# Moving the global-by-global scores of an attention kernel into the spare columns of another score bank

## The chip, the cores and the metric

The kernel runs on one core of a Trainium2 chip. The metric is the device time of one execution in microseconds. An execution of this kernel is one launch that takes 64 attention heads and a gated feed-forward layer from inputs in HBM to outputs in HBM. The core's engines are named as in the profile: PE does matrix multiplies (its weight loads have their own row, PEld), DVE and ACT do elementwise work and can read PSUM, POOL does elementwise work in SBUF only, and SP issues DMAs.

## The reference

There are 8 batches of 8 heads, 512 local tokens, 32 global tokens and a head dimension of 64. A local token attends to the 32 global keys and to local keys within 32 positions. A global token attends to all 32 + 512 keys. The result is a token's input to a gated feed-forward layer of 512 to 1536 to 512.

```python
k_all = np.concatenate([k_g, k_l], axis=2)
s_g = scale * np.matmul(q_g, k_all.transpose(0, 1, 3, 2))   # global queries: 32 x 544 scores a head
out_g = np.matmul(sm(s_g), v_all)
...
mask = np.abs(pos[:, None] - pos[None, :]) <= window        # local queries: a band, plus the globals
s_l = np.concatenate([s_lg, s_ll], axis=-1)
out_l = np.matmul(sm(s_l), v_all)
...
gate = 1.0 / (1.0 + np.exp(-(x @ w_gate)))
return gate * (x @ w_val) @ w_out
```

## The kernel before, in words

Everything is computed to float32 accuracy. Operands are split into a high and a low float32r part (`qk_hi` and `kl`, `vhl`, `xt`, `hh`), and a product takes two or three matmuls. Weights come as float64 words and are converted at the start (`convert`).

The work is cut into chunks of tokens: two half chunks of batch 0, then one chunk of 512 local tokens for each of the batches 1 to 7, and at last the global tokens of all batches. The feed-forward of one chunk (`ffn_stream`) walks over 12 blocks of the hidden dimension. A block has 12 matmuls into `bank_g`, 12 into `bank_v` and 12 into the output banks `bank_o`. Between groups of these matmuls runs the attention of the next chunk, so attention of the chunks for batches 2 to 7 (six of them) runs under a steady feed-forward, and attention of batch 0 and 1 runs at the start, among the weight conversion.

A head of a full chunk has three attention units: `local_unit` for query blocks 0 and 1, `local_unit` for query blocks 2 and 3 (the second local unit), and `global_unit`. Each unit has four stages:

- Local: scores into a bank `bank_x` of shape [128, 2, 256], of which a block uses 224 columns (`WIN`); mask and row maximum on DVE (line 237), exponent on ACT (line 240). Then the normalisation into `p_buf` on DVE (line 213). Then four transposes on PE into `bank_y` (line 254), whose two float32r parts are made by ACT (line 263) and DVE (line 264, the tile `pt`). Then the product with the values (lines 280 and 281), and `t0` and the sum of parts on ACT, DVE and POOL.
- Global: scores with the local keys into `sa`, a `bank_x` of [32, 4, 128] (line 299), and scores with the 32 global keys into `sb`, a `bank_y` of its own of [32, 32] (line 301). DVE takes the row maximum of both (lines 304 and 305) and combines them (line 306), ACT takes the exponents of both (lines 308 and 309) into `pg_buf`, DVE scales it (lines 311 to 313), PE transposes it (line 317).

The feed-forward's own elementwise work for a block of the hidden dimension: tanh of `bank_g` on ACT (line 370), minimum on DVE (375), absolute value (377) and exponent (376) on ACT, `th` from two SBUF operands on DVE (378), times `bank_v` on DVE (380), the split of `hh` on ACT (382) and POOL (383). The split of the next heads' queries and keys is a cast on ACT (193) and three subtractions on POOL (194 and 196).

PSUM has eight banks. Four hold `bank_o`. The other four are one pool, which `bank_x`, `bank_y`, `bank_g` and `bank_v` share:

```python
acc = ps.tile([P, 512], F32, name=nm, tag="att", bufs=4)[:, 0:ntok]
s_ps = ps.tile([P, 2, 256], F32, name="bank_x", tag="att", bufs=4)
sb = ps.tile([32, 32], F32, name="bank_y", tag="att", bufs=4)
```

A tile of the pool gets its bank when an earlier tile's last reader is done, and PE waits for that reader.

The order of the work comes from two things. The driver emits stages of attention by ticks of the feed-forward (one tick is four matmuls of 512 columns): units follow each other every 4 ticks and a unit's stages lie 3 ticks apart. A block of the hidden dimension has 9 ticks and a head has 12, so the position of a head within the feed-forward repeats every three heads; from tick 8 of a chunk on everything is put off by one tick. From what is emitted the framework makes each engine's queue, in an order that it plans when the program is built. An engine works through its queue strictly in that order.

Of the kernel before, what the change touches and what calls it, by code (L numbers as in the profile page):

```python
# [8 lines left out]
F32 = mybir.dt.float32  # L9
# [11 lines left out]
SG = 32  # L21
NH = 8
# [4 lines left out]
QK = Q1 + 256 + SG  # L27
VM = (0, 1, 4, 5)
VS = (2, 3, 6, 7)
WIN = 224  # L30
DM = 512

# Where work is issued, in ticks of the feed-forward (one tick is four 512-token
# matmuls). Attention units of a chunk follow each other every PER ticks; a unit's
# stages lie STAGES apart, its operands are loaded and split ahead of it.
BASE, PER = 3, 4
STAGES = (0, 3, 6, 9)
LOAD_QK, LOAD_V, SPLIT_QK, SPLIT_V = 16, 9, 10, 4
LOAD_V_NATIVE = 4
# from the first of these ticks of a chunk on, attention is put off by the second  # L40
HOLE = (8, 1)
START = dict(per0=4, base1=1, per1=1.1, base2=23, per2=3, x2=28, lead=8, native_heads=4)
CONVERT = (-2, 4, 1, 3)
CONVERT_EARLY = (-985, -980, -977)
# the engines that share a kind of operation in turn: v(ector), s(calar)
NORM = {0: "v", 1: "v", 2: "ssv", 3: "sv"}
# [4 lines left out]
KT = DM // P  # L51
# [3 lines left out]
def kernel(ctx, tc, qk, v, w_gate, w_val, w_out, out_l, out_g):  # L55
    nc = tc.nc
# [4 lines left out]
    const = ctx.enter_context(tc.tile_pool(name="const", bufs=1))  # L61
    raw = ctx.enter_context(tc.tile_pool(name="raw", bufs=1))
    spl = ctx.enter_context(tc.tile_pool(name="spl", bufs=2))
    att = ctx.enter_context(tc.tile_pool(name="att", bufs=2))
# [5 lines left out]

# [1 line left out]
    ident = const.tile([P, P], F32, name="ident")  # L72
# [3 lines left out]
    nc.gpsimd.memset(masks[:, 1], 0.0)  # L76
    # window column c < 96 stands for key c - 32, c >= 128 for key c - 64
    # (relative to the block's first query); the columns between are global
    mid = masks[:, 1]
    for c0, lo, hi in ((0, 0, 64), (128, 96, -32)):  # L80
        cols = mid[:, c0:c0 + 96]
# [12 lines left out]
    pg = const.tile([32, 5 * P], F32, name="pg_buf")  # L94
    nc.vector.memset(pg, 0.0)
    xg32 = const.tile([P, KT, NG], F32, name="xg32")

# [1 line left out]
    wg = [const.tile([P, KT, DF], F32R, name=f"wg{i}") for i in range(2)]  # L99
# [19 lines left out]
    def convert(i, hi, lo):  # L119
        """The two float32r parts of a float64 [128, KT or 1, n] block, given as words."""  # L120
        src = w_src[i]
        t, n = src.shape[1], src.shape[2] // 2
        st, v = (o[i % len(o)].rearrange("p (t n) -> p t n", t=t) for o in conv_bufs)
        words = st.rearrange("p t (n two) -> p t n two", two=2)
        low, high = words[:, :, :, 0], words[:, :, :, 1]
        vf, hf = v.bitcast(F32), high.bitcast(F32)
        with tc.issue_after(anchor[0].ins) if i < 3 else nullcontext():
            nc.vector.tensor_scalar(v, high, 0x80000000, None, op0=ALU.bitwise_and)
            # read as a float32, the high word times 2^-112 has its exponent rebased to
            # float32's, with zeros between the sign and the exponent's eight bits  # L130
            if REBASE[i % len(REBASE)] == "s":
                nc.scalar.mul(hf, hf, 2.0 ** -112)
            else:
                nc.vector.tensor_scalar(hf, hf, 2.0 ** -112, None, op0=ALU.mult)
            nc.vector.scalar_tensor_tensor(v, low, 29, v, op0=ALU.logical_shift_right, op1=ALU.bitwise_or)
            nc.vector.scalar_tensor_tensor(v, high, 3, v, op0=ALU.logical_shift_left, op1=ALU.bitwise_or)
        nc.scalar.copy(hi, vf)
        nc.gpsimd.tensor_tensor(lo, vf, hi.bitcast(F32), op=ALU.subtract)
        stage(i + len(conv_bufs[0]))
# [11 lines left out]

# [1 line left out]
    def qcol(j):  # L153
# [62 lines left out]
    def local_unit(T, blocks, x32s, h, col0):  # L216
        ks, k0s, q0 = T["qk"], T["k0"], T["q0"]
        nat = T["native"]
        last = len(ks) - 1
        s_ps = ps.tile([P, 2, 256], F32, name="bank_x", tag="att", bufs=4)  # L220
        for i, j in enumerate(blocks):
            qj = ks[0][:, qcol(j) - q0:qcol(j) - q0 + P]
            for t, (kt, k0) in enumerate(zip(ks, k0s)):
                js = slice(k0 + j * BLK, k0 + j * BLK + WIN)
                nc.tensor.matmul(s_ps[:, i, 0:WIN], qj, kt[:, js], start=t == 0, stop=t == last)  # L225
# [9 lines left out]
        for i, j in enumerate(blocks):  # L235
            m = 0 if j == 0 else (2 if j == 3 else 1)
            anchor[0] = nc.vector.tensor_tensor_reduce(  # L237
                out=s_sb[:, i], in0=s_ps[:, i, 0:WIN], in1=masks[:, m], scale=-0.125, scalar=3.0e38,
                op0=ALU.add, op1=ALU.min, accum_out=nm[:, i:i + 1])
            nc.scalar.activation(s_sb[:, i], s_sb[:, i], AF.Exp, bias=nm[:, i:i + 1], scale=-1.0,  # L240
                                 accum_out=sm[:, i:i + 1])
        yield
        nc.vector.tensor_scalar_add(r, sm, 1e-9)  # L243
# [43 lines left out]
    def global_unit(T, b, h):  # L287
# [5 lines left out]
        sa = ps.tile([32, 4, P], F32, name="bank_x", tag="att", bufs=4)  # L293
        sb = ps.tile([32, 32], F32, name="bank_y", tag="att", bufs=4)
        for half in range(2):
            o0 = 96 * half
            for t, (src, k0) in enumerate(zip(ks, k0s)):
                view = src[:, k0 + 32:k0 + 32 + 4 * BLK].rearrange("p (j c) -> p j c", c=BLK)[:, :, o0:o0 + 64]
                nc.tensor.matmul(sa[:, :, 64 * half:64 * half + 64], qg, view, start=t == 0, stop=t == last)  # L299
        for t, (src, k0) in enumerate(zip(ks, k0s)):  # L300
            nc.tensor.matmul(sb, qg, src[:, k0 + 96:k0 + 128], start=t == 0, stop=t == last)  # L301
        mg = small.tile([32, 4], F32, name="mg")
# [35 lines left out]

# [1 line left out]
    hl_q = []  # L340
# [6 lines left out]
    def ffn_stream(items):  # L347
        """Items (chunk, block of the hidden dimension); yields the part of a full
        512-token step that was issued, between groups of matmuls."""
        prev = None  # L350
# [57 lines left out]

    # ---- driver: attention of the next chunk runs between the matmul groups
    def att_events(ci, start, per, tail=0):  # L410
        """(tick, order, thunk) of all attention work for chunk ci."""
        b, blocks, with_g = chunks[ci]
# [8 lines left out]
        for h in range(NH):  # L421
            native = ci + 1 if ci < 2 or (ci == 2 and h < START["native_heads"]) else 0
            place = (spl, "qk_hi", QK)
            if ci == 0 and h >= 4:
                place = (spl, "kl", KEXT)
            if ci == 1 and h // 2 == 2:
                place = (raw, "qk_raw", QK)
            heads.append(dict(first=ci == 0, native=native, h=h, n=b * NH + h, cols=slice(c0, c1),
                              wins=slice(0, 8 if with_g else 4), group=group, place=place))
# [38 lines left out]
    chs.append(dict(ntok=NG, x0=0, o0=0, first=False, xt=lambda: xts[G], dst=out_g))  # L468
    # the first two half chunks share the steps in which the weights are converted
    lead = START["lead"]  # L470
# [5 lines left out]

    # events on the feed-forward's clock: one tick is four 512-token matmuls
    queue = att_events(0, -1000, START["per0"]) + att_events(1, START["base1"], START["per1"])
# [85 lines left out]
```

## Time and profile before

| | |
|---|---|
| median of 3 runs | 1266.98 us (1265.59 to 1267.98) |
| span of the profiled execution | 1265.6 us |
| PE busy | 1221.5 us, 97% |
| DVE, ACT, POOL busy | 877.6 us (69%), 783.3 us (62%), 570.6 us (45%) |
| start, until attention of batch 1 is done | about 270 us |
| a steady chunk | 139.2 us, six of them with attention |
| the last full chunk, feed-forward alone, and the global tokens | about 160 us |

The span is the profiled execution's own time; it lies 1.4 us below the median. In the views that follow a row of the timeline gives start and duration in us, engine, line, operation, what is written and read, the shape, and in brackets the idle time of the engine before it with what ended it. A busy PE is not a PE at its peak: its matmuls are pipelined, so the distance between two starts tells what a matmul costs.

### The profile page before, as it was taken

Reading aid. Unit: us, or ns where it says so; the run is one execution under the profiler, and the core shown is the slowest. Engines: PE = TensorE matmul, PEld = TensorE weight load, DVE = VectorE, ACT = ScalarE, POOL = GpSimd, SP = SyncE. Lnnn points to the kernel's source line nnn. Section 1 sums busy time; section 2 is a strip of 40 time slices with the busy share of each in tenths; the row PEclk is TensorE's granted clock in tenths of the full one; section 3 lists DMA queues with packets and bytes.
Section 4 is the critical chain, followed back from the end, with each engine's and each line's share of the span. In section 5 each row is a group of like instructions: output and inputs, shape, how many; then the busy total and the mean of one; then the engine's idle time right before and its main releaser. Section 6 shows DMA issues by size and latency. Waiting matters only on the chain.

```text
span 1265.6 us, 20474 instructions
## 1 busy us (share of the span) xinstructions
PE 1221.5 (97%) x6820; PEld 994.1 (79%) x6820; DVE 877.6 (69%) x2433; ACT 783.3 (62%) x1899; POOL 570.6 (45%) x573
## 2 busy tenths in 40 slices
PE   5899989999999999999999999999999999999998
PEld 4676768788788877888788877888788877888897
DVE  4797976757877777857876778767775787632232
ACT  4586766756666666666666667756765766532233
POOL 1444554545555355545555455535554555311111
PEclk9698999999999999999999999999999999999999
DMA  5576864333333333333333423343334332122143
GB/s 198 197 259 225 254 191 145 92 121 99 92 107 98 115 99 108 91 121 108 107 92 107 126 78 107 109 127 111 92 86 126 116 92 87 44 90 67 67 133 117
DMA packets 59497, 151.90 MB, mean 120 GB/s; under 512 B 6144, under 2 KB 19456, under 8 KB 59392
## 3 DMA queue, kind: packets, MB, share of 16 engines
q1 hardware_dynamic: 59392, 150.59, 38.9%
q8 instruction: 54, 0.88, 0.3%
q14 instruction: 51, 0.42, 0.1%
HBM read 135.36 MB, written 15.20 MB: 119 GB/s over the span
## 4 chain that ended last, share of the span: by engine, by line
PE 77%; DVE 13%; ACT 5%; issue 3%; POOL 1%; DMA 1%; SPq 0%; POOLq 0%; DVEq 0%; ACTq 0%
PE bank_g L362 20%; PE bank_v L362 19%; PE bank_o L396 19%; PE bank_x L225 5%; PE bank_y L254 4%; DVE p_buf L213 3%; DVE th L378 2%; PE bank_y L317 2%; PE bank_x L330 2%; PE bank_x L280 2%; PE bank_x L299 2%; PE bank_x L281 1%; DVE pg_buf L213 1%; ACT s_sb L240 1%; DVE pt L264 1%
## 5 line engine op out<-in xcount | busy, mean ns | idle before, releaser
L362 PE MATMUL bank_g<-xt,wg 128*128 128x512 f32 (+1 forms) x1440 | 340.3, 371 | 1.8 <-DVE th L380 1.8
L362 PE MATMUL bank_v<-xt,wv 128*128 128x512 f32 (+1 forms) x1440 | 332.6, 368 | 3.0 <-DVE pt L264 2.7
L396 PE MATMUL bank_o<-wo,hh 128*128 128x512 f32 x1224 | 334.0, 404 | 0.8 <-ACT hh L382 0.4
L362 PEld LDWEIGHTS bank_g<-xt,wg 128*128 128x128 f32 x1440 | 238.6, 192 | 41.6 <-issue 3.4
L362 PEld LDWEIGHTS bank_v<-xt,wv 128*128 128x128 f32 x1440 | 237.8, 190 | 40.7 <-PE bank_y L301 3.1
L396 PEld LDWEIGHTS bank_o<-wo,hh 128*128 128x128 f32 x1224 | 214.1, 189 | 38.9 <-ACT hh L382 1.2
L383 POOL TENSOR_TENSOR hh<-th,hh 128x512 fp32r<-128x512 f32 (+1 forms) x120 | 137.6, 1147 | 199.7 <-ACT hh L382 198.8
L240 ACT ACTIVATE s_sb<-s_sb,nm 128x224 f32<-128x224 f32 x240 | 113.8, 475 | 143.1 <-DVE nm L237 142.0
L213 DVE TENSOR_SCALAR p_buf<-s_sb,r 128x128 f32<-128x128 f32 (+1 forms) x443 | 151.8, 386 | 4.2 <-PE bank_y L254 0.4
L375 DVE TENSOR_SCALAR mn<-bank_g 128x512 f32<-128x512 f32 (+1 forms) x108 | 67.3, 623 | 110.7 <-ACT th L370 109.3
L378 DVE SCALAR_TENSOR_TENSOR th<-th,mn 128x512 f32<-128x512 f32 (+1 forms) x120 | 101.5, 846 | 59.0 <-ACT mn L376 52.7
L285 POOL TENSOR_TENSOR x<-t 64x256 f32<-64x256 f32 x104 | 76.4, 734 | 142.8 <-DVE t L284 138.7
L194 POOL TENSOR_TENSOR kl<-qk_raw,qk_hi 128x704 fp32r<-128x704 f32 x52 | 88.4, 1701 | 114.8 <-ACT qk_hi L193 114.8
L370 ACT ACTIVATE th<-bank_g 128x512 f32<-128x512 f32 (+1 forms) x120 | 63.5, 529 | 97.7 <-PE bank_g L362 96.1
L382 ACT CAST hh<-th 128x512 fp32r<-128x512 f32 (+1 forms) x120 | 66.5, 554 | 68.1 <-DVE th L380 67.3
L237 DVE CUSTOM_DVE_ANT_0 s_sb<-bank_x,masks 128x224 f32<-128x224 f32 x240 | 83.8, 381 | 12.7 <-PE bank_x L225 8.4
L254 PE MATMUL bank_y<-ident,p_buf 128*128 128x128 f32 x496 | 80.1, 282 | 10.8 <-DVE p_buf L213 6.6
L196 POOL TENSOR_TENSOR qk_hi<-qk_raw,qk_hi 64x256 fp32r<-64x256 f32 x104 | 87.7, 863 | 4.1
L254 PEld LDWEIGHTS bank_y<-ident,p_buf 128*128 128x128 f32 x496 | 60.9, 143 | 32.5 <-ACT pg_buf L308 6.6
L243 DVE TENSOR_SCALAR r<-sm 128x2 f32<-128x2 f32 x128 | 29.3, 229 | 75.5 <-ACT s_sb L240 74.2
L193 ACT CAST qk_hi<-qk_raw 128x1248 fp32r<-128x1248 f32 x52 | 64.1, 1233 | 22.2 <-PE bank_y L301 22.1
L380 DVE TENSOR_TENSOR th<-bank_v,th 128x512 f32<-128x512 f32 (+1 forms) x120 | 72.4, 604 | 5.1 <-PE bank_v L362 1.3
(109 smaller groups left out, 1985.9 us busy)
## 6 DMA issues: line engine op xcount, KB each, us to landing
wo<-wo_dram SPq DMA_DIRECT2D x116, 512.0 KB, 3.5
qk_raw<-in_qk_dram SPq DMA_DIRECT2D x104, 312.0 KB, 4.4
v_raw<-in_v_dram SPq DMA_DIRECT2D x52, 256.0 KB, 2.6
out_dram<-ob SPq DMA_DIRECT2D x34, 256.0 KB, 3.0
xt<-in_w_gate_dram SPq DMA_DIRECT2D x12, 512.0 KB, 4.5
xt<-in_w_val_dram SPq DMA_DIRECT2D x12, 512.0 KB, 4.4
xt<-in_w_out_dram SPq DMA_DIRECT2D x12, 512.0 KB, 4.9
v_nat<-in_v_dram SPq DMA_DIRECT2D x8, 512.0 KB, 5.5
```

Of the source, the lines that this page charges most:

```text
L194: nc.gpsimd.tensor_tensor(kl, t[:, K0:Q1], hi[:, K0:Q1].bitcast(F32), op=ALU.subtract)
L196: nc.gpsimd.tensor_tensor(hi[64:128, r], t[64:128, r], hi[64:128, r].bitcast(F32), op=ALU.subtract)
L213: nc.vector.tensor_scalar(out, in_, by, None, op0=ALU.mult)
L237: anchor[0] = nc.vector.tensor_tensor_reduce(out=s_sb[:, i], in0=s_ps[:, i, 0:WIN], in1=masks[:, m], scale=-0.125, scalar=3.0e38, op0=ALU. ...
L240: nc.scalar.activation(s_sb[:, i], s_sb[:, i], AF.Exp, bias=nm[:, i:i + 1], scale=-1.0, accum_out=sm[:, i:i + 1])
L254: nc.tensor.transpose(pt_ps[:, 2 * i + t], pb[:, i, t * P:(t + 1) * P], ident)
L285: nc.gpsimd.tensor_tensor(dst, t0[:, :, 0], t0[:, :, 1], op=ALU.add)
L362: nc.tensor.matmul(acc, w[a][:, t, fs], xt[:, c, t, x0:x0 + ntok], start=n == 0, stop=n == 11)
L378: nc.vector.scalar_tensor_tensor(th, th, 1.0, mn, op0=ALU.add, op1=ALU.mult)
L380: nc.vector.tensor_tensor(th, acc, th, op=ALU.mult)
L383: nc.gpsimd.tensor_tensor(hh[:, 1, 0:ntok], th, hh[:, 0, 0:ntok].bitcast(F32), op=ALU.subtract)
L396: nc.tensor.matmul(o_ps[t], ph[:, a, t * P:(t + 1) * P], pwo[:, c], start=f2 == 0 and i == 0, stop=f2 == NF - 1 and i == 2)
```

## The change

The 32 x 32 scores of the global queries with the global keys no longer have a bank of their own. The second local unit of a head issues them ahead of its own scores, into the 32 columns of its score bank that block 0 leaves free, and behind its exponents ACT copies them to `gg_sb` in SBUF. The global unit reads them there: the maximum on DVE and the exponent on ACT have an SBUF operand in place of a PSUM operand.

```diff
+    gg_sb = const.tile([SG, 2, SG], F32, name="gg_sb")
...
 def local_unit(T, blocks, x32s, h, col0):
...
         s_ps = ps.tile([P, 2, 256], F32, name="bank_x", tag="att", bufs=4)
+        with_gg = T["with_g"] and blocks[-1] == 3
+        if with_gg:
+            gg = s_ps[0:SG, 0, WIN:]
+            for t, (kt, k0) in enumerate(zip(ks, k0s)):
+                nc.tensor.matmul(gg, ks[0][:, QK - SG - q0:QK - q0], kt[:, k0 + 96:k0 + 128],
+                                 start=t == 0, stop=t == last)
         for i, j in enumerate(blocks):
...
                                  accum_out=sm[:, i:i + 1])
+        if with_gg:
+            nc.scalar.copy(gg_sb[:, h % 2], gg)
         yield
...
 def global_unit(T, b, h):
...
-        sb = ps.tile([32, 32], F32, name="bank_y", tag="att", bufs=4)
...
-        for t, (src, k0) in enumerate(zip(ks, k0s)):
-            nc.tensor.matmul(sb, qg, src[:, k0 + 96:k0 + 128], start=t == 0, stop=t == last)
+        sb = gg_sb[:, h % 2]
...
-            heads.append(dict(first=ci == 0, native=native, h=h, n=b * NH + h, cols=slice(c0, c1),
+            heads.append(dict(first=ci == 0, with_g=with_g, native=native, h=h, n=b * NH + h, cols=slice(c0, c1),
```

No tick changes, but the planned queues do. In a steady chunk PE's queue differs at the moved pair of every head and otherwise only at the third and sixth head. Line numbers of the changed kernel are 8 to 10 higher (254 becomes 264, 264 becomes 274, 280 becomes 290, 362 becomes 370).

First, PE's queue at the global unit of the third and sixth head, before: the pair of line 301, then the matmuls of `bank_v` with the local unit's value product in between. The four transposes come behind all twelve.

```order
L299 MATMUL bank_x<-kl,qk_hi 32x4x64
L301 MATMUL bank_y<-qk_hi 32x32
L301 MATMUL bank_y<-kl,qk_hi 32x32
L362 MATMUL bank_v<-xt,wv_113 128x512 x4
L362 MATMUL bank_v<-xt,wv_114 128x512 x3
L280 MATMUL bank_x<-pt,vhl 128x256
L281 MATMUL bank_x<-pt,vhl 128x256
L280 MATMUL bank_x<-pt,vhl 128x256
L281 MATMUL bank_x<-pt,vhl 128x256
L362 MATMUL bank_v<-xt,wv_114 128x512
L362 MATMUL bank_v<-xt,wv_113 128x512 x4
```

And the same place now:

```order
L308 MATMUL bank_x<-kl,qk_hi 32x4x64
L370 MATMUL bank_v<-xt,wv_114 128x512 x4
L290 MATMUL bank_x<-pt,vhl 128x256
L291 MATMUL bank_x<-pt,vhl 128x256
L290 MATMUL bank_x<-pt,vhl 128x256
L291 MATMUL bank_x<-pt,vhl 128x256
L370 MATMUL bank_v<-xt,wv_115 128x512 x4
L264 MATMUL bank_y<-ident,p_buf 128x128 x4
L370 MATMUL bank_v<-xt,wv_114 128x512 x4
```

The value product has moved three matmuls ahead and the transposes four.

Second, ACT's queue at the same heads, before, from the exponents of the second local unit on (`th` is the feed-forward's tile; line 193 is the cast of a later head's queries and keys):

```order
L240 ACTIVATE s_sb,sm<-s_sb,nm 128x224 x2
L335 COPY y<-bank_x 64x64
L205 CAST vhl<-v_raw 128x8x64
L263 CAST pt<-bank_y 128x512
L370 ACTIVATE th<-bank_g 128x512
L377 ACTIVATE th<-th 128x512
L193 CAST qk_hi<-qk_raw 128x1248
L376 ACTIVATE mn<-mn 128x512
```

And now:

```order
L248 ACTIVATE s_sb,sm<-s_sb,nm 128x224 x2
L251 COPY gg_sb<-bank_x 32x32
L343 COPY y<-bank_x 64x64
L206 CAST vhl<-v_raw 128x8x64
L273 CAST pt<-bank_y 128x512
L378 ACTIVATE th<-bank_g 128x512
L194 CAST qk_hi<-qk_raw 128x1248
L385 ACTIVATE th<-th 128x512
L384 ACTIVATE mn<-mn 128x512
```

The copy has come in behind the exponents, and the cast has changed places with the absolute value of `th`.

Third, DVE's queue at the same heads, before, from the maximum over `sa` to the next local unit's mask:

```order
L304 TENSOR_REDUCE mg<-bank_x 32x1
L375 TENSOR_SCALAR mn<-bank_g 128x512
L305 TENSOR_REDUCE mg<-bank_y 32x1
L306 TENSOR_SCALAR mg<-mg 32x1
L378 SCALAR_TENSOR_TENSOR th<-th,mn 128x512
L311 TENSOR_SCALAR mg<-sg 32x1
L380 TENSOR_TENSOR th<-bank_v,th 128x512
L284 TENSOR_TENSOR t_6981<-bank_x,t_6981 64x512
L264 TENSOR_TENSOR pt<-bank_y,pt 128x512
L312 RECIPROCAL mg<-mg 32x1
L213 TENSOR_SCALAR pg_buf<-pg_buf,mg 32x576
L237 ISA s_sb,nm<-bank_x,masks 128x224
```

And now:

```order
L312 TENSOR_REDUCE mg<-bank_x 32x1
L383 TENSOR_SCALAR mn<-bank_g 128x512
L314 TENSOR_SCALAR mg<-mg 32x1
L386 SCALAR_TENSOR_TENSOR th<-th,mn 128x512
L319 TENSOR_SCALAR mg<-sg 32x1
L320 RECIPROCAL mg<-mg 32x1
L214 TENSOR_SCALAR pg_buf<-pg_buf,mg 32x576
L294 TENSOR_TENSOR t_6982<-bank_x,t_6982 64x512
L274 TENSOR_TENSOR pt<-bank_y,pt 128x512
L388 TENSOR_TENSOR th<-bank_v,th 128x512
L245 ISA s_sb,nm<-bank_x,masks 128x224
```

The scaling of `pg_buf` has moved ahead of `t0` and `pt`, and the product of `th` with `bank_v` behind them. The small maximum has left this stretch: in every steady head it now stands further ahead, between the sum `r` of the second local unit and its reciprocal, where it waits for the copy on ACT. At the start of the program (attention of batch 0 and the first heads of batch 1, among the weight conversion) the queues of PE, DVE and ACT differ in many more places.

## The prediction

> **What bounds the kernel now.** I read the page's busy times first, then one steady chunk by window, then PE's waits between 400 and 1100 us, then the timeline at the places that these waits name.
>
> ```profile
> span 1265.6 us, 20474 instructions
> PE 1221.5 (97%) x6820; PEld 994.1 (79%) x6820; DVE 877.6 (69%) x2433; ACT 783.3 (62%) x1899; POOL 570.6 (45%) x573
> 545.69:684.88 139.19, 137.82 (x754) 112.26 (x753) 104.66 (x296) 92.24 (x214) 71.77 (x72) 1.00 0.36 106
> PE bank_x L280 <- DVE pt L264: 2.9, 7, 0.5
> PE bank_v L362 <- DVE pt L264: 2.2, 5, 0.4
> PE bank_y L317 <- DVE pg_buf L213: 1.0, 5, 0.2
> ```
>
> PE is the bound: in a chunk of 139.19 us it is idle 1.37 us. What it waits for is always DVE, though DVE is busy only three quarters of the chunk (104.66 us). So the change can win what these waits cost, and it can lose wherever DVE or ACT get later. Moving or removing PE work wins nothing here: the pair of small matmuls stays, in another place.
>
> An idle time understates a wait, since the start that comes late also costs the overlap with the matmul before. So I price waits from start to start. The sixth head of a chunk, then the fourth:
>
> ```profile
> 505.83 0.68 DVE L264 TENSOR_TENSOR pt<-bank_y,pt 128x512 fp32r<-128x512 f32 x1
> 506.04 0.18 PE L301 MATMUL bank_y<-kl,qk_hi 128*32 128x32 f32 x1
> 506.66 0.47 PE L362 MATMUL bank_v<-xt,wv 128*128 128x512 f32 x1 [0.44 <-DVE pt L264]
> ...
> 511.81 1.10 PE L396 MATMUL bank_o<-wo,hh 128*128 128x512 f32 x4
> 512.75 0.28 PE L280 MATMUL bank_x<-pt,vhl 128*128 128x256 f32 x1
> 513.22 1.08 PE L396 MATMUL bank_o<-wo,hh 128*128 128x512 f32 x4
> 514.23 0.49 PE L317 MATMUL bank_y<-ident,pg_buf 32*128 32x32 f32 x5
> ...
> 612.63 0.18 PE L301 MATMUL bank_y<-kl,qk_hi 128*32 128x32 f32 x1
> 612.66 1.19 PE L396 MATMUL bank_o<-wo,hh 128*128 128x512 f32 x4
> 614.37 0.36 PE L280 MATMUL bank_x<-pt,vhl 128*128 128x256 f32 x1 [0.52 <-DVE pt L264]
> ```
>
> Unhindered, the step behind line 301 takes 0.03 us (612.63 to 612.66), four matmuls and the step to line 280 take 0.94 us (511.81 to 512.75), and to line 317 1.01 us. So `bank_v` in the sixth head pays 0.62 - 0.03 = 0.59 us: it needs the bank of the transposes that line 264 reads until 506.51. The fourth head's line 280 pays 1.71 - 1.01 = 0.70 us. Now the third head:
>
> ```profile
> 596.61 0.63 ACT L377 ACTIVATE th<-th 128x512 f32<-128x512 f32 x1
> 597.14 1.22 ACT L193 CAST qk_hi<-qk_raw 128x1248 fp32r<-128x1248 f32 x1
> 598.44 1.71 POOL L194 TENSOR_TENSOR kl<-qk_raw,qk_hi 128x704 fp32r<-128x704 f32 x1 [2.06 <-ACT qk_hi L193]
> 598.99 1.70 DVE L378 SCALAR_TENSOR_TENSOR th<-th,mn 128x512 f32<-128x512 f32 x1 [0.99 <-ACT mn L376]
> 601.47 1.11 PE L396 MATMUL bank_o<-wo,hh 128*128 128x512 f32 x4
> 602.01 0.67 DVE L264 TENSOR_TENSOR pt<-bank_y,pt 128x512 fp32r<-128x512 f32 x1
> 602.74 0.38 PE L280 MATMUL bank_x<-pt,vhl 128*128 128x256 f32 x1 [0.16 <-DVE mg L312]
> 602.78 1.67 DVE L213 TENSOR_SCALAR pg_buf<-pg_buf,mg 32x576 f32<-32x576 f32 x1
> 602.86 1.28 POOL L383 TENSOR_TENSOR hh<-th,hh 128x512 fp32r<-128x512 f32 x1
> 603.31 1.09 PE L396 MATMUL bank_o<-wo,hh 128*128 128x512 f32 x4
> 604.38 0.37 DVE L237 CUSTOM_DVE_ANT_0 s_sb<-bank_x,masks 128x224 f32<-128x224 f32 x1
> 604.60 0.46 PE L317 MATMUL bank_y<-ident,pg_buf 32*128 32x32 f32 x5 [0.20 <-DVE pg_buf L213]
> ```
>
> Line 280 pays 1.27 - 0.94 = 0.33 us and line 317 pays 1.29 - 1.01 = 0.28 us. These rows show what makes DVE late: an operation with SBUF operands alone ends only behind the POOL operation that it meets. `th` (598.99) ends at 600.69, 0.54 us behind line 194 on POOL; `pg_buf` (602.78) ends at 604.45, 0.31 us behind line 383. Operations that read PSUM (`pt`, 0.67 and 0.68 us) are not stretched.
>
> All four places together cost 0.59 + 0.70 + 0.33 + 0.28 = 1.90 us a chunk. There are six steady chunks with attention, so 11.4 us is the most to be won there.
>
> **The change part by part.** The prices of the small operations:
>
> ```profile
> L305 DVE TENSOR_REDUCE mg<-bank_y x64: 158/169/172, 58.4 to 1095.4; 32x1 f32<-32x32 f32 x64
> L335 ACT COPY y<-bank_x x52: 208/208/210, 222.2 to 1105.8; 64x64 f32<-64x64 f32 x52
> L244 DVE RECIPROCAL r<-r x128: 143/166/177, 13.0 to 1091.8; 128x2 f32<-128x2 f32 x128
> ```
>
> *The pair of matmuls.* It has the same shapes, so PE work is unchanged: zero, either way a few hundredths of a microsecond. In its new place it needs the queries, keys and bank that the scores behind it need anyway, so it adds no wait.
>
> *The copy on ACT.* 64 copies of about 0.21 us (line 335 is the nearest row) make 13 us of ACT, which has 47 us free in every chunk. In the queue it delays what follows by 0.1 to 0.2 us: the casts of `vhl` and `pt`, tanh and the exponent that `th` waits for.
>
> *The maximum over `gg_sb`.* It costs what it cost (0.17 us) but waits for the copy, and behind it on DVE stand the reciprocal and four scalings into `p_buf`. So these come 0.2 to 0.4 us later, and what follows `sa` comes 0.2 us earlier. In the fourth head DVE has 0.23 us of idle time ahead of `th` (612.34, below) that takes most of this. I book +0.1 us at each of two heads where the value product has no slack, +0.2 us a chunk.
>
> [...] If the reduce behaved like line 213 it would cost up to 1.2 us more wherever it meets POOL, and the sum below would lose its sign.
>
> *The bank.* `sb` held a bank from line 301 until ACT had read it. Now the score bank of the second local unit is held about 0.2 us longer, until the copy; the `sa` that takes it follows 16 feed-forward matmuls behind the scores, some 3.8 us at the 0.94 us for four. I take the wait as covered by these; without that cover the copy's 0.2 us would fall on PE in eight heads. The `bank_v` of the sixth head no longer needs the transposes' bank: -0.59 us a chunk. What is late next there is line 280, which I follow now.
>
> *The new order at the third and sixth head.* On ACT the cast takes the place of the absolute value, 0.53 us earlier (597.14 - 596.61), and the exponent behind both stays where it is. So POOL's line 194 runs 597.91 to 599.62, and `th` ends 0.54 us behind it, at 600.15 in place of 600.69. The two small operations follow, then `pg_buf` starts near 600.43, while POOL is in the first of its two line 196 (from 599.70; each takes 0.86 us at 617.19 below, and this one a little more, since it meets `th`: to 600.6 or 600.8). Where does `pg_buf` get in? The rows nearest:
>
> ```profile
> 617.19 1.71 POOL L196 TENSOR_TENSOR qk_hi<-qk_raw,qk_hi 64x256 fp32r<-64x256 f32 x2
> 617.27 0.97 DVE L213 TENSOR_SCALAR pg_buf<-pg_buf,mg 32x576 f32<-32x576 f32 x1
> 227.95 1.49 POOL L196 TENSOR_TENSOR qk_hi<-qk_raw,qk_hi 64x256 fp32r<-64x256 f32 x2
> 228.64 1.11 DVE L213 TENSOR_SCALAR pg_buf<-pg_buf,mg 32x576 f32<-32x576 f32 x1
> 225.91 0.39 PE L280 MATMUL bank_x<-pt,vhl 128*128 128x256 f32 x1 [0.76 <-DVE pt L264]
> 227.97 0.66 PE L254 MATMUL bank_y<-ident,p_buf 128*128 128x128 f32 x4 [0.38 <-ACT pg_buf L308]
> PE bank_g L362 <- DVE th L380: 1.8, 1, 1.8
> ```
>
> At 617.27 it ended at 618.24, between the two; at 228.64, with the first about to end, it ended at 229.75, behind both. I take the first, since 600.43 lies 0.2 to 0.4 us ahead of the switch: end near 601.0, then `t0` and `pt` (0.67 at most each) end near 602.3. PE is ready for line 280 at 601.47 + 0.94 = 602.41 in the third head, and in the sixth, moved by the 0.59 us, at 602.35 on the same scale. So both waits of the third head go (-0.61 us) and the sixth head keeps its -0.59 us. Behind both POOL operations `pt` would end at 603.1: +0.1 us in the third head and +0.2 us in the sixth in place of the gain.
>
> *The fourth head.* Its two rows:
>
> ```profile
> 608.41 0.39 DVE L237 CUSTOM_DVE_ANT_0 s_sb<-bank_x,masks 128x224 f32<-128x224 f32 x1
> 612.34 1.28 DVE L378 SCALAR_TENSOR_TENSOR th<-th,mn 128x512 f32<-128x512 f32 x1 [0.23 <-ACT mn L376]
> ```
>
> Behind the third head DVE is early: `pt` ends near 602.3, the product of `th` takes 0.6, and the next mask comes near 602.9 in place of 604.38. The mask at 608.41, which begins the way to the fourth head's late `pt`, is further back in that queue and can come earlier by some of this 1.5 us, but not ahead of its scores. Between -0.70 us and +0.2 us; I take -0.3, because the copy, and POOL's `hh` that now comes later, push against it.
>
> Sum of a steady chunk: -0.61 - 0.59 - 0.3 + 0.2 = -1.3 us, times six: -7.8 us.
>
> *The heads between 200 and 262 us* (batch 1's last four): line 254 waits for a bank that ACT releases, 0.38 us; now it waits for one that is free. Line 280 ahead of it (0.76 us) gets 0.1 later by the copy. -0.2 us each: -0.8 us.
>
> *The start.* Order changes all over, and its waits for banks are long (1.8 us in this row), but DVE is close to full. From -4 to +4 us; I take -0.5.
>
> Total -9.1 us on 1265.6 gives 1256.5 for the profiled execution, which lies 1.4 below the median of the runs: 1258 us.
>
> **The rivals.** *Caught behind both POOL operations, or given back:* the waits of the third and sixth head return a little longer, the fourth head keeps its own: (0.1 + 0.2 + 0.2) x 6 = +3.0 us, less 0.8 and 0.5 at the start: 1268.7 against 1267, within 0.2% (2.5 us, about what a measurement can tell from no change). For it: 228.64. Against it: nearly all other meetings end like 617.27.
>
> *Only the bank counts:* the sixth head gains 0.59 us and the rest cancels: 6 x 0.59 + 0.8 = 4.3 us, 1262.7. For it: the bank is all that the edit itself frees.
>
> *Slower: DVE's new wait reaches PE.* Every wait of PE is for DVE, and eight heads a chunk now hold DVE 0.2 us for the copy. If the new order saves nothing and this arrives at PE in all: 8 x 0.2 x 6 = 9.6 us, less 3.5 for the bank: 1273. It decides from about 0.13 us a head upward. Against it: DVE idles 34 us a chunk, and the maximum behind `sa` has gone.
>
> **How the numbers follow.** The forecast has 0.58, the bank alone 0.14, the given-back case 0.15, the slower one 0.13. Faster: 0.58 + 0.14 = 0.72. The range goes from the forecast with the whole fourth head and a good start (-0.4 x 6 - 3: 1252.5) to the edge of the given-back case, 1266.
>
> **What would show it.** Right: in the sixth head `bank_v` follows line 308 without idle time; at the third and sixth head `pg_buf` on DVE ends between POOL's two subtractions; line 325 waits no more; a chunk takes about 137.9 us. Wrong: `pg_buf` of 1.1 us or more behind both subtractions, line 290 idle at heads that had none, or a start that ends later than 270 us by more than the chunks win.

## The result, and the profile after

The changed kernel takes 1275.1 us (median of 4 executions, 1271.83 to 1278.63) against 1267.17 us for the kernel before on the same chip: 1.0062 of its time, with an interval of 1.0039 to 1.0085. It is slower, where 1258 us was forecast with a range of 1252.5 to 1266. Most kernels here, the one before included, have some executions about 5 us longer than their others (two of the four of the changed kernel, but none of the profiled ones; the change held in the old order to the end also has one of 1668 us), so where a median mixes the two kinds I go by the profiled execution. Between these the change costs 5.5 us (spans of 1271.1 and 1265.6).

First the page's first lines of the profile after, then the third full steady chunk by window (columns: length, busy time of PE, PE's loads, DVE, ACT, POOL, then granted clock, DMA share and GB/s), and PE's waits from 400 to 1100 us (sum, times, longest):

```profile
span 1271.1 us, 20545 instructions
PE 1224.5 (96%) x6820; PEld 995.9 (78%) x6820; DVE 859.1 (68%) x2433; ACT 786.1 (62%) x1963; POOL 569.6 (45%) x573
556.51:694.48 137.97, 137.37 (x753) 112.00 (x753) 100.85 (x296) 92.55 (x222) 71.80 (x72) 1.00 0.36 106
PE bank_x L290 <- DVE pt L274: 3.0, 11, 0.5
```

The chunk that took 139.19 us takes 137.97, close to the 137.9 forecast. Of the groups of waits there only the one ahead of line 290 (line 280 before) is left. So the steady chunks did what was expected. The loss lies ahead of them. The group of twelve matmuls into `bank_o` that opens a chunk stands, before and after, at

```profile
406.45 3.06 PE L396 MATMUL bank_o<-wo,hh 128*128 128x512 f32 x12
418.34 3.03 PE L404 MATMUL bank_o<-wo,hh 128*128 128x512 f32 x12
```

That is 11.9 us later, although one shorter chunk, 1.2 us of gain, already lies ahead of it. The start has lost 13.1 us. Its waits of PE between 60 and 280 us, the largest six:

```profile
PE bank_y L264 <- DVE p_buf L214: 5.0, 2, 4.6
PE bank_y L264 <- ACT p_buf L212: 4.8, 1, 4.8
PE bank_y L325 <- DVE pg_buf L214: 4.4, 3, 2.8
PE bank_y L264 <- ACT gg_sb L251: 1.8, 3, 0.8
PE bank_x L290 <- DVE pt L274: 1.2, 4, 0.5
PE bank_x L308 <- DVE th L386: 1.2, 1, 1.2
```

The longest wait there was 1.8 us before. Now there are waits of 4.8, 4.6 and 2.8 us for the scalings into `p_buf` and `pg_buf`, and only 1.8 us in all for the copy. One of the long waits, in the rows of ACT, DVE and PE that lead to it:

```profile
152.63 0.18 ACT L248 ACTIVATION_READ_ACCUMULATOR s_sb<-s_sb,nm 128x1 f32 x1
152.82 0.68 DVE L137 SCALAR_TENSOR_TENSOR xt<-xt 128x512 uint32<-128x512 uint32 x1
...
154.43 1.77 DVE L136 SCALAR_TENSOR_TENSOR xt<-xt 128x512 uint32<-128x512 uint32 x1
156.12 0.96 DVE L129 TENSOR_SCALAR xt<-xt 128x512 uint32<-128x512 uint32 x1
157.00 1.30 DVE L137 SCALAR_TENSOR_TENSOR xt<-xt 128x512 uint32<-128x512 uint32 x1
158.22 1.21 DVE L136 SCALAR_TENSOR_TENSOR xt<-xt 128x512 uint32<-128x512 uint32 x1
159.36 1.23 DVE L253 TENSOR_SCALAR r<-sm 128x2 f32<-128x2 f32 x1
...
162.33 0.69 ACT L212 ACTIVATE p_buf<-s_sb,r 128x128 f32<-128x128 f32 x2
162.78 0.69 PE L264 MATMUL bank_y<-ident,p_buf 128*128 128x128 f32 x2 [4.76 <-ACT p_buf L212]
```

The sums of the exponents are there at 152.81. The operation on them stands on DVE behind eight others, seven of them steps of the weight conversion (`xt`), and starts 6.5 us later. Four of these steps (from 154.43 on) take 0.96 to 1.77 us, where the one at 152.82 takes 0.68; POOL is at work from 154.23 to 160.56 almost without a gap. So part of the 6.5 us looks like the stretching that the prediction read in the steady chunks. PE's queue has the transposes of `p_buf` ahead of feed-forward work, so PE stands. Nothing in these rows is an operation of the change; what is new is the order.

The idle time is only a little more than half of the loss. By window (same columns), first the start as a whole before and after, then three stretches of after that follow such waits:

```profile
0.00:270.00 270.00, 238.99 (x1498) 189.06 (x1499) 205.97 (x590) 178.35 (x510) 121.56 (x120) 0.94 0.59 189
0.00:270.00 270.00, 231.81 (x1405) 180.84 (x1406) 199.68 (x577) 172.12 (x505) 110.60 (x110) 0.90 0.58 184
165.00:170.00 5.00, 5.00 (x19) 4.15 (x19) 4.76 (x13) 1.68 (x4) 1.29 (x1) 0.50 0.96 337
190.00:195.00 5.00, 5.00 (x16) 3.46 (x17) 2.23 (x10) 2.25 (x7) 1.62 (x1) 0.50 0.66 190
195.00:200.00 5.00, 5.00 (x19) 3.57 (x18) 0.70 (x3) 1.55 (x5) 0.72 (x1) 0.50 0.10 22
```

PE is idle 7.2 us more (238.99 - 231.81). The other 6 us of the 13.1 are left for busy time at a lower clock: behind the waits that end at 162.78 and 188.23 the granted clock is 0.50. Eight matmuls of one shape show what that does, at 0.50 and once it is back:

```profile
192.38 2.07 PE L370 MATMUL bank_v<-xt,wv 128*128 128x256 f32 x8
194.38 0.69 PE L284 MATMUL bank_x<-pt_nat,v_nat 128*64 128x128 f32 x2
...
202.27 1.22 PE L370 MATMUL bank_g<-xt,wg 128*128 128x256 f32 x8
203.42 0.77 PE L338 MATMUL bank_x<-ptg_nat,v_nat 128*64 128x32 f32 x10
```

From start to the next start they take 2.00 us against 1.15.

### The profile page after: what moved, and what is told of

Read it like the earlier page. It is cut to its first block, busy times and chain, and to the rows that moved or that the text cites. A ratio compares the mean times of both kernels' runs of the same rounds, so it can differ in the third digit from the quotient of the medians.

```text
span 1271.1 us, 20545 instructions
## 1 busy us (share of the span) xinstructions
PE 1224.5 (96%) x6820; PEld 995.9 (78%) x6820; DVE 859.1 (68%) x2433; ACT 786.1 (62%) x1963; POOL 569.6 (45%) x573
## 4 chain that ended last, share of the span: by engine, by line
PE 69%; DVE 8%; ACT 6%; issue 2%; DMA 1%; POOLq 0%; POOL 0%; DVEq 0%; ACTq 0%; SPq 0%
PE bank_g L370 19%; PE bank_o L404 18%; PE bank_v L370 17%; PE bank_x L233 3%; PE bank_y L264 3%; DVE th L386 2%; PE bank_x L290 2%; PE bank_x L338 2%; PE bank_x L291 2%; PE bank_y L325 2%; ACT s_sb L248 1%; PE bank_x L308 1%; DVE pt L274 1%; DVE p_buf L214 1%; ACT mn L384 1%
## 5 line engine op out<-in xcount | busy, mean ns | idle before, releaser
L370 PE MATMUL bank_v<-xt,wv 128*128 128x512 f32 (+1 forms) x1440 | 337.8, 371 | 0.1
L391 POOL TENSOR_TENSOR hh<-th,hh 128x512 fp32r<-128x512 f32 (+1 forms) x120 | 138.0, 1150 | 215.6 <-ACT hh L390 215.4
L214 DVE TENSOR_SCALAR p_buf<-s_sb,r 128x128 f32<-128x128 f32 (+1 forms) x443 | 148.3, 380 | 5.1 <-PE bank_y L264 1.6
L386 DVE SCALAR_TENSOR_TENSOR th<-th,mn 128x512 f32<-128x512 f32 (+1 forms) x120 | 93.1, 776 | 61.8 <-ACT mn L384 56.0
L253 DVE TENSOR_SCALAR r<-sm 128x2 f32<-128x2 f32 x128 | 33.9, 265 | 79.4 <-ACT s_sb L248 77.3
```

The lines of the kernel that those rows point to most:

```text
L214: nc.vector.tensor_scalar(out, in_, by, None, op0=ALU.mult)
L370: nc.tensor.matmul(acc, w[a][:, t, fs], xt[:, c, t, x0:x0 + ntok], start=n == 0, stop=n == 11)
L386: nc.vector.scalar_tensor_tensor(th, th, 1.0, mn, op0=ALU.add, op1=ALU.mult)
L391: nc.gpsimd.tensor_tensor(hh[:, 1, 0:ntok], th, hh[:, 0, 0:ntok].bitcast(F32), op=ALU.subtract)
```

## Experiments

The theory after the result (A): the steady win is real, and the loss is the order that the planner gives the start once the operations of the change are in it. Its rivals: the shorter chunks are an effect of another phase (B); the new operations cost a price per head where DVE and ACT are nearly full (C). "First twelve" is the start of the `bank_o` group above, "chunk" the mean of the five distances between such groups from there on, both in us and in the profiled execution. Of the profiled execution of the kernel before the span alone is known; in the others the time lies 1.8 to 2.1 us above the span.

| kernel | median us | ratio to before, interval | profiled us | first twelve | chunk |
|---|---|---|---|---|---|
| before | 1266.8 to 1267.2 | 1 | span 1265.6, so about 1267.5 | 406.45 | 139.2 |
| the change | 1275.10 | 1.0062 (1.0039 to 1.0085) | 1272.95 | 418.34 | 138.0 |
| from batch 2 on | 1259.79 | 0.9951 (0.9933 to 0.9969) | 1260.29 | 405.05 | 138.0 |
| and batch 1's last four heads | 1259.54 | 0.9953 (0.9936 to 0.9970) | 1258.50 | 403.27 | 138.0 |
| batch 0 alone | 1270.30 | 1.0024 (1.0012 to 1.0036) | 1271.41 | 410.31 | 139.3 |
| batch 1 alone | 1265.66 | 0.9994 (0.9979 to 1.0009) | 1266.85 | 405.45 | 139.2 |
| the change, start in the old order | 1258.82 | 0.9946 (0.9925 to 0.9967) | 1259.03 | 403.88 | 138.0 |
| the change, all in the old order | 1271.61 | 1.0035 (1.0022 to 1.0048) | 1267.34 | 406.19 | 139.2 |
| bank of its own, copied | 1263.39 | 0.9975 (0.9957 to 0.9993) | 1262.68 | 404.88 | 138.5 |
| spare columns, no copy | 1274.25 | 1.0052 (1.0032 to 1.0072) | 1270.07 | 405.29 | 139.9 |
| before, tick 22.5 | 1268.35 | 1.0011 (0.9996 to 1.0026) | 1268.18 | 405.39 | 139.5 |
| before, tick 23.5 | 1269.76 | 1.0034 (1.0017 to 1.0051) | 1269.24 | 406.65 | 139.5 |
| the change, tick 22.5 | 1263.18 | 0.9967 (0.9948 to 0.9986) | 1261.88 | 406.91 | 138.0 |
| the change, tick 23.5 | 1264.70 | 0.9986 (0.9968 to 1.0004) | 1262.95 | 408.11 | 138.0 |

**The steady chunks alone.** A condition chooses by chunk which of the two ways the pair goes; the same condition serves the next three runs.

```diff
-        with_gg = T["with_g"] and blocks[-1] == 3
+        with_gg = T["gg"] and blocks[-1] == 3
...
-            heads.append(dict(first=ci == 0, with_g=with_g, native=native, h=h, n=b * NH + h, cols=slice(c0, c1),
+            heads.append(dict(first=ci == 0, gg=with_g and (ci >= 3), native=native, h=h, n=b * NH + h, cols=slice(c0, c1),
...
-        sb = gg_sb[:, h % 2]
+        sb = gg_sb[:, h % 2] if T["gg"] else ps.tile([32, 32], F32, name="bank_y", tag="att", bufs=4)
...
+        if not T["gg"]:
+            for t, (src, k0) in enumerate(zip(ks, k0s)):
+                nc.tensor.matmul(sb, qg, src[:, k0 + 96:k0 + 128], start=t == 0, stop=t == last)
```

> The change is made for the six chunks from batch 2 on alone; the attention of batches 0 and 1 keeps the separate bank, and its instructions stand in the order of the kernel before. Theory A (the steady chunks win what was forecast, and the whole loss lies ahead of 270 us, where the new operations changed the planned order): the bank_o group of twelve that stands at 406.52 us before comes near 405.3, the chunks behind it take 137.9 us, and the time is 1267.2 - 6 x 1.25 = 1259.7 us. Theory B (the steady chunks look shorter only because the start left them in another phase): the chunks take about 139.2 us again and the time is 1267.

1259.79 us, with the group of twelve at 405.05 and 138.0 us a chunk. Theory A has it to a tenth; B falls. Ahead of 270 us every queue stands here as in the kernel before, so this kernel also says what the change would have brought with an unharmed start.

**With batch 1's last four heads** (`ci >= 3 or ci == 2 and not native`):

> As the run with the change from batch 2 on, and also for the last four heads of batch 1 (200 to 262 us). By the prediction these four heads win 0.2 us each: 0.8 us less than the run beside it, near 1258.9 us. The rival, from the profile after (three waits of PE for a bank that the copy holds, 0.39 to 0.83 us, and waits behind line 290 that are shorter by about as much): no difference from the run beside it, 1259.7 us.

The medians (1259.54 and 1259.79) can't tell the two; in the profiled executions the group of twelve comes 1.8 us earlier. Between 195 and 270 us PE waits 1.9 us for banks that the copy holds, but its waits ahead of line 290 are 0.9 us in place of 3.2. I leave the size open; a loss it is not.

**Batch 0 alone and batch 1 alone** (`ci == 1`; `ci == 2`):

> The change for the eight global heads of batch 0 alone (attention up to about 130 us). Theory A (the planned order): the price is not one per head but hangs on where single operations fall; PE's new waits of over 1 us lie mostly behind 130 us, so this part costs little, between -2 and +5 us: 1265 to 1272 us. Theory C (a fixed price per head: the copy on a full ACT and the wait for it on a full DVE, some 15 us over 16 heads, 0.9 us each): +7 us, 1274 us.

> The change for the eight heads of batch 1 alone (about 130 to 262 us), its start up to the first of these being ordered as before. Theory A: the order between 130 and 200 us is planned anew, PE gets waits of 3 to 5 us for the scalings into p_buf, and a lower granted clock behind them: +6 to +14 us, 1273 to 1281 us. Theory C: +7 us, 1274 us, spread over the heads in waits of under 1 us each.

Batch 0 alone costs 3.5 us by the medians, within A's range. Batch 1 alone costs nothing, which A had at 6 to 14 us and C at 7: both were wrong on it. The two parts move the group of twelve by +3.9 and -1.0 us against before; both together, which is the start of the changed kernel, by +13.3 against the steady chunks alone (418.34 - 405.05). No price per head adds up like that, so C as put is out, and so was my placing of the harm in batch 1's operations. What fits is an order that comes out another way for each combination.

**The order held in the start.** The whole change, but the instructions ahead of the first steady chunk are bound by ordering edges to the order of the kernel before, on all five queues; a table lists it.

```diff
+    for engine, text in HELD.items():
...
+        before = None
+        for part in text.split():
...
+                    if before is not None:
+                        tc.add_manual_dep(
+                            ins, before.name,
+                            mybir.DependencyInfo(mybir.DependencyClass.NoSync, mybir.DependencyReason.DATA),
+                            reason="order held")
+                    before = ins
```

> The whole change, but ahead of the first steady chunk every engine's instructions are held in the order of the kernel before (ordering edges alone, no waits); the new pair of matmuls stands just ahead of the scores of its unit, the copy just behind the exponents of its unit. Theory A (the loss of the start is the new order and nothing else): PE's waits of 3 to 5 us between 140 and 190 us are gone, the group of twelve stands near 405, and the time is that of the run with the steady chunks alone, 1259.8 us, give or take 1.5. Theory C (the new instructions themselves delay DVE and ACT where both are nearly full): the loss stays in the old order too, 1270 us or more.

1258.82 us, the lowest median here. The same instructions as in the changed kernel, all 64 copies among them, and the start's 13 us are gone. Its waits of PE between 60 and 270 us, the two largest, and the window of the start:

```profile
PE bank_y L319 <- DVE p_buf L270: 4.2, 3, 2.2
PE bank_x L345 <- DVE pt L329: 1.8, 4, 0.9
0.00:270.00 270.00, 237.18 (x1507) 185.75 (x1508) 205.95 (x590) 180.58 (x529) 120.81 (x120) 0.96 0.60 191
```

No wait is over 2.2 us and the granted clock is 0.96, where the changed kernel had 0.90. A is shown: order alone makes the loss, and C, with its 1270 us or more, is out for good.

**The order held to the end.** The same with the table for the whole program, which leaves the change its bank and its copy and takes its order away.

> The whole change with the order of the kernel before held on every engine to the end. It tells the bank from the order in the steady chunks. Theory A (as the prediction's terms have it): the sixth head wins its 0.59 us, since the bank is free, the third and fourth heads keep their waits, the copy costs 0 to 0.2 us: chunks of 138.6 to 138.8 us and 1267 - 6 x 0.5 = 1264 us. Rival (the bank is all): chunks of 137.9 us and 1259.8 us. Rival (the order is all): 139.2 us and 1267 us.

The chunks take 139.2 us and the profiled execution 1267.34 us, as before the change: "the order is all" has it, my own terms don't. This reading rests on the chunks and the profiled execution; by the medians this kernel lies 0.35% above before. In one chunk, the third, fourth and sixth head (line 440 is the value product, 280 of before):

```profile
602.77 0.39 PE L440 MATMUL bank_x<-pt,vhl 128*128 128x256 f32 x1 [0.36 <-DVE pt L424]
...
614.47 0.36 PE L440 MATMUL bank_x<-pt,vhl 128*128 128x256 f32 x1 [0.45 <-DVE pt L424]
...
650.01 1.10 PE L554 MATMUL bank_o<-wo,hh 128*128 128x512 f32 x4
651.46 0.39 PE L440 MATMUL bank_x<-pt,vhl 128*128 128x256 f32 x1 [0.35 <-DVE pt L424]
```

The wait for `bank_v` in the sixth head is gone and its 0.59 us won. Then the next value product of that head pays 1.45 - 0.94 = 0.51 us, which it did not before: DVE is as late as ever, and PE meets it one step further on. So the free bank is worth nothing by itself in this order.

**What the spare columns and the copy are for.** From batch 2 on alone, first with the pair in a bank of its own, then with no copy, the maximum and the exponent reading PSUM.

```diff
-            gg = s_ps[0:SG, 0, WIN:]
+            gg = ps.tile([SG, SG], F32, name="bank_y", tag="att", bufs=4)
```

```diff
-            nc.scalar.copy(gg_sb[:, h % 2], gg)
+            T["gg_ps"] = gg
```

> From batch 2 on alone: the pair is issued early, ahead of the scores of the second local unit, but into a bank of its own, copied to SBUF as in the change. So a fifth tenant of the four shared banks lives from there to the copy, some 2 us. Theory A (a shorter way through the banks is half of the steady win): it is given back, chunks of 138.6 to 139.5 us, 1264 to 1269 us. Rival (what counts is only that the pair and its read leave the global unit): 137.9 us a chunk, 1260 us.

> From batch 2 on alone: the pair goes into the spare columns, but nothing is copied; the maximum and the exponent read PSUM. So the score bank of the second local unit is held until the last exponent of the global unit, some 5 us longer, eight times a chunk. Theory A: PE waits for the four shared banks, at least 0.3 us a head: 1267 + 6 x (8 x 0.3 - 0.6) = 1278 us or more. Rival (a bank is mostly free in these stretches): 1258 to 1262 us, since the copy and the wait for it are saved.

With its own bank a chunk takes 138.5 us, so half of the steady win is given back, the size that was expected, with the time 0.6 us better than my range. Without the copy a chunk takes 139.9 us, 0.8 worse than before the change; the direction is A's, but I had more than twice the size. PE's waits from 405 to 1100 us, first with the bank of its own, then the largest without the copy:

```profile
PE bank_x L290 <- DVE pt L274: 4.0, 6, 0.9
PE bank_y L264 <- DVE mn L386: 6.4, 10, 0.7
```

Neither run shows the bank alone. With its own bank PE waits for no bank at all, only for `pt`, which line 290 reads, about once a chunk; what moved in the queues of a steady chunk is the copy, now ahead of the exponents on ACT, and the maximum on DVE. So my range held by luck: the way through the banks was not what gave the half back. Without the copy PE does wait for a bank, that of `bank_g`, until the minimum on DVE has read it. But in its queues at the third and sixth head the value product on PE and the scaling of `pg_buf` on DVE stand where they stood before the change, so this kernel has lost the new order too, and the two causes are not parted.

**The start as a draw.** One number of the start is moved, which plans the queues anew between about 125 and 270 us and leaves the steady chunks' instructions in their order: in the kernel before, and in the changed one.

```diff
-START = dict(per0=4, base1=1, per1=1.1, base2=23, per2=3, x2=28, lead=8, native_heads=4)
+START = dict(per0=4, base1=1, per1=1.1, base2=22.5, per2=3, x2=28, lead=8, native_heads=4)
```

> The kernel before, unchanged but for one number: the attention of batch 1 is put at tick 22.5 in place of 23, which gives the planner another order between some 125 and 270 us and leaves the steady chunks as they were. Theory A (the start is a draw of the order, in which the kernel before holds a lucky one): slower by 2 to 12 us, 1269 to 1279 us, with new waits of over 1 us for the scalings into p_buf or pg_buf. Rival (an order planned anew costs nothing by itself; only the changed instructions upset it): within 2 us of 1267.

> The kernel before with the attention of batch 1 at tick 23.5 in place of 23. Theory A: slower by 2 to 12 us, 1269 to 1279 us, by another sum of waits than at 22.5. Rival: within 2 us of 1267.

> The whole change with the attention of batch 1 at tick 22.5. The steady chunks keep their 138 us. Theory A: a new draw, which after so unlucky a one is likelier better than worse: 1260 to 1272 us, waits of 4 to 5 us at other places or gone. Rival (the changed instructions cost some 13 us of the start in any planned order): 1270 to 1275 us.

> The whole change with the attention of batch 1 at tick 23.5. Theory A: a new draw, 1260 to 1272 us. Rival: 1270 to 1275 us.

The kernel before gets 1.3 and 2.7 us slower, the first less than A had, and not to be told from no change. Nor is it the start that got slower: the group of twelve stands at 405.39 and 406.65, against 406.45. The excess lies in the steady chunks, 139.5 us in place of 139.2, with their queues in the same order. There PE's waits for `pt` have grown from 2.9 us (405 to 1105 us, first at tick 22.5, then at 23.5):

```profile
PE bank_x L280 <- DVE pt L264: 4.2, 11, 0.8
PE bank_x L280 <- DVE pt L264: 4.4, 11, 0.8
```

Why is open. So A's lucky start of the kernel before is not shown, and a chunk in one and the same order can differ by 0.3 us, a quarter of what the change wins there.

The changed kernel gets 10 to 11 us faster by either shift (profiled executions), and at 22.5 it beats the kernel before (0.9967). So the order that the change got at tick 23 is the bad draw: of the five kernels that have the change in all of batch 0, batch 1 or both, in an order of the planner's own, four have the group of twelve at 405.5 to 410.3 us, and it alone at 418.3. With the 1.2 us of the first chunk taken off, the two shifted starts are still 1.7 and 2.9 us longer than that of the kernel before; whether the change's operations cost that in most orders, these few draws don't tell.

## Why the prediction was wrong, step by step

**The steady chunk** was forecast at -1.3 us and came at -1.2 (139.19 to 137.97; 6 chunks bring 7 us in the run with these alone). By its steps: the sixth head's `bank_v` no longer waits, as forecast. The third head's rows in the profile after:

```profile
609.04 1.70 POOL L195 TENSOR_TENSOR kl<-qk_raw,qk_hi 128x704 fp32r<-128x704 f32 x1 [1.54 <-ACT qk_hi L194]
610.47 0.82 DVE L386 SCALAR_TENSOR_TENSOR th<-th,mn 128x512 f32<-128x512 f32 x1 [1.41 <-ACT mn L384]
610.82 2.05 POOL L197 TENSOR_TENSOR qk_hi<-qk_raw,qk_hi 64x256 fp32r<-64x256 f32 x2
611.63 0.57 DVE L214 TENSOR_SCALAR pg_buf<-pg_buf,mg 32x576 f32<-32x576 f32 x1
612.54 1.10 PE L404 MATMUL bank_o<-wo,hh 128*128 128x512 f32 x4
613.48 0.35 PE L290 MATMUL bank_x<-pt,vhl 128*128 128x256 f32 x1
614.03 1.09 PE L404 MATMUL bank_o<-wo,hh 128*128 128x512 f32 x4
615.05 0.49 PE L325 MATMUL bank_y<-ident,pg_buf 32*128 32x32 f32 x5
```

`th` ends 0.55 us behind line 195, and `pg_buf` gets in between POOL's two subtractions, with 0.57 us in place of 1.67. Line 290 comes 0.94 us behind its matmuls and line 325 1.02 us: the two waits of 0.33 and 0.28 us are gone, as forecast. The fourth head, and the seventh, which waits anew:

```profile
623.22 1.09 PE L404 MATMUL bank_o<-wo,hh 128*128 128x512 f32 x4
624.49 0.36 PE L290 MATMUL bank_x<-pt,vhl 128*128 128x256 f32 x1 [0.17 <-DVE pt L274]
...
670.72 1.07 PE L404 MATMUL bank_o<-wo,hh 128*128 128x512 f32 x4
672.11 0.36 PE L290 MATMUL bank_x<-pt,vhl 128*128 128x256 f32 x1 [0.32 <-DVE pt L274]
```

The fourth pays 1.27 - 0.94 = 0.33 us in place of 0.70: -0.37, where -0.3 was taken. The seventh pays 1.39 - 0.94 = 0.45 us, which it did not before, where +0.2 was taken for the new wait of DVE; that it is the copy which makes it late is not shown. Sum: -0.59 - 0.61 - 0.37 + 0.45 = -1.12.

**The bank as a term of its own** was wrong though the sum was right. The prediction priced it apart from the order, and made a rival of it (1262.7 us). The run with the old order to the end shows it at nothing. The prediction did ask what is late next, and answered with times of the new order; the run shows no gain from the free bank without that order.

**The heads between 200 and 262 us**, -0.8: not settled by the times, in the profiled executions rather more. The way there was another: line 264 (254 before) does not find a free bank but waits for the copy, and the gain is ahead of line 290.

**The start is the step that failed.** It was put at -4 to +4 us, with -0.5 taken, and measured +13.1. Two things were missing. The bound of 4 us was made from the longest wait of the kernel before, 1.8 us, as if a new order could only move waits of the kind already there; but a wait for `p_buf` can be as long as the run of conversion steps that the planner puts ahead of it on DVE: 6.5 us of them, and a wait of 4.76 us, in the rows above. And behind such waits (4.8 and 4.6 us) PE worked on at a granted clock of 0.50, where eight matmuls of one shape took 2.00 us in place of 1.15. That the order of the start changed all over was seen, and then booked as if good and bad would cancel. In the old order the start comes to the forecast number: the group of twelve at 403.88 against 406.45 is -2.6 us, of which -1.2 belong to the first chunk, -1.4 to the start and the heads behind it (-1.3 forecast), and the time is 1258.8 us, against the forecast 1258. That the start hits it is luck: ahead of 270 us PE is busy for 237.18 us in place of 238.99, so it idles more and not less, and the gain goes with a granted clock of 0.96 in place of 0.94.

The prediction's slower rival (1273 us) came near the time by another way: it had DVE's wait for the copy reach PE in every head of the steady chunks. These got shorter.

## What to carry to other kernels

Where a planner sets the order, an edit is two changes: what it does, and the new order of everything near it. Price them apart, and where queues are nearly full, give the new order a range from the longest run of other work that can be put ahead of a waited-for operation, not from the waits already there; then measure the edit with the old order held, or only where the order stays good. And a freed bank or a removed wait is worth nothing until it is shown, in the order that will run, that the next operand is ready.

## What was not expected of the hardware

The price of a long wait of PE can be more than its length. After waits of 4.8 and 4.6 us the granted clock was 0.50 for whole stretches of 5 us, and the same eight matmuls took 2.00 in place of 1.15 us; of the start's 13.1 us some 6 are left for this, beside 7.2 of idle time. With PE busy throughout (5.00 us in each window of 5), the clock was still 0.50 from 190 to 200 us. How long a wait brings it down is not shown: in the kernel before the clock fell behind waits of 1.8 us at most (0.58 in this window):

```profile
178.00:182.00 4.00, 3.47 (x17) 3.47 (x17) 2.13 (x8) 3.05 (x9) 2.16 (x3) 0.58 0.20 75
```

That the maximum over `gg_sb` would cost what it cost from a bank (0.17 us) was an estimate: no row of the kernel before has a reduce from SBUF. It was never stretched (169 ns at most, nine of the 64 beginning while POOL was at work), so the doubt that the prediction kept there did not come true, and what it read of `th` and `pg_buf` beside POOL does not hold for every operation with SBUF operands alone: one of the nine ran from 187.16 to 187.31 us, beside an operation of POOL from 186.74 to 188.00. Another operation of that size was stretched: the one on 128x2 elements that ends at 160.59 us took 1.23 us while POOL ran from 159.03 to 160.56. The rows:

```profile
L313 DVE TENSOR_REDUCE mg<-gg_sb x64: 152/167/169, 53.7 to 1097.7; 32x1 f32<-32x32 f32 x64
L253 DVE TENSOR_SCALAR r<-sm x128: 149/170/1226, 12.7 to 1097.6; 128x2 f32<-128x2 f32 x128
159.03 1.53 POOL L139 TENSOR_TENSOR wv<-xt,wv 128x512 fp32r<-128x512 f32 x1
```
